# Dense first layer with products alternating between two PSUM banks, and rounding, lo parts and cuts issued one or two products later

## The chip, the cores and the metric

One core of one Trainium2 chip. The number is device time in microseconds; lower is better. Five engines run their own instruction streams in order and wait for one another through semaphores: TensorE (PE; its weight loads PEld), VectorE (DVE), ScalarE (ACT), GpSimd (POOL) and SyncE (SP), which here mostly starts DMAs.

## The reference

Three layers in a row, float32 throughout, with large inputs (most are drawn 8 times wider), so that products are computed in split precision.

```python
k_p, v_p = mean of k, v over groups of 8 positions            # pooled attention
attn = softmax(q @ k_p.T / sqrt(D)) @ v_p                     # 8 x 8 heads, 576 x 64
x = attn as (4608, 512)
e = argmax(x @ w_gate); x = gate * sigmoid(...) * relu(x @ w1[e]) @ w2[e]   # 8 experts
h = x @ w_in                                                  # (4608, 512) @ (512, 2048)
r = maximum(h, 0); g = s * (r * r) + b
out = g @ w_out                                               # (4608, 2048) @ (2048, 512)
```

The last three lines are the dense stage, the one that is mostly changed.

## The kernel before

The program runs attention, then the expert stage, then the dense stage. Every engine's order is written out by hand, in the order of the Python calls; nothing moves instructions afterwards.

**Split precision.** A float32 factor is kept as a rounded part (hi, made on ScalarE by an activation with `Copy`) and a rest (lo, made on VectorE by subtracting hi). A product is three matmuls: hi x hi, hi x lo, lo x hi. `split` (L806 to L808) makes one pair; where the raw values are features or weights, the text calls it a cut.

**Dense stage** (class `Dense`). Tokens come in 6 groups of 768, the 2048 hidden features in 8 pairs of 128 columns, so there are 48 steps, counted `n = 8 q + p`. The first layer of a step is Winograd's form of a 2 x 2 block product: seven products of 384 columns (six matmuls each, lines 1339 to 1341) instead of eight. They take seven sums of feature blocks (`xt`, cut once a group) and seven sums of weight blocks (`ws`, in DRAM, read back through a ring of 8 slots). The table `PROD` gives, for each product, the weight sum, the PSUM bank and whether the bank starts anew. After a product, `post` reads its bank: `keep` copies it (ScalarE, L1345, for products 0, 2 and 3), or `finish` completes one quarter of the hidden values: addition of a kept block on VectorE (L1359) or Relu on ScalarE (L1355), square (L1361 or L1357), scale and bias on VectorE (L1362), rounding on ScalarE (L1368), and the lo part (L1350) at the next finish. The second layer of step n-1 runs as 12 chunks (three matmuls of 512 columns each, L1315 to L1317) placed after the products of step n by `AFTER`; they accumulate in six further PSUM banks (`po`) and are copied and stored by POOL's indirect DMA at the end of a group (L1324 to L1327).

The features of the next group are prepared meanwhile: `load` (transposing DMAs, L1229), `join` on POOL (two halves put together, L1248, and a multiplication by the token's scale, L1252), the sums on POOL (L1255), and seven `cut`s in the group's last step and the next one's first. Two of POOL's four sums are made in `cut`, after the cuts that read the blocks they overwrite.

**Weights.** `Doubles.step` turns the 64-bit `w_in` and `w_out` into float32. In the expert stage it forms the sums of `w_in`, cuts them into `halves()`, one buffer, and in the next call stores that to `ws` from SP's queue (L925). Two pieces out of four end in such a cut. Twelve pieces of `w_out` are left for the first dense steps.

**End of the expert stage.** After slot 35 there may be more slots under conditions on the number of tiles; `ahead` issues POOL's joins and sums for the first group just before them. The gathers of later slots (L1012) follow on POOL.

## Time and profile before

| | us |
|---|---|
| three runs, median (range) | 1550.47 (1550.26 to 1553.07) |
| profiled execution | 1553.91 |
| its span, first to last instruction | 1552.0 |
| TensorE busy | 1441.0 (93%) |
| VectorE / ScalarE / POOL busy | 919.1 / 536.8 / 563.9 (59% / 35% / 36%) |
| mean granted TensorE clock | 0.983 |

Matmuls overlap in the pipeline and their ends are modelled, so the busy share of TensorE says little by itself; the time between starts and the waits say more. Attention lasts to about 300 us, the expert stage to about 711 us, the dense stage's first product starts at 712.8 us. Steps are counted by their products: line 1339 has 672 matmuls, 14 in each of 48 steps.

### The profile page before, as it was taken

The page shows a single profiled execution, that of the slowest core. Times are in us where ns is not written, and L with a number is a line of the kernel's source. Part 1 is how long each engine was busy: PE and PEld are TensorE (multiplying, and loading weights), DVE is VectorE, ACT ScalarE, POOL GpSimd, SP SyncE. Part 2 cuts the span into 40 slices and gives each one's busy share as a digit, 9 for nine tenths or more (in the row PEclk, how much of TensorE's full clock was granted, in tenths as well). Part 3 has the DMA queues.
Part 4 walks back from the last instruction along what each step waited for, and adds up shares of the span by engine and source line. Part 5 has one row for each costly group of instructions (what it writes and reads, how often), then busy time and mean ns, then how long its engine had stood idle before and what let it go on. Part 6 is the DMA issues. An engine that isn't in the chain of part 4 may idle for free.

```text
span 1552.0 us, 23038 instructions
## 1 busy us (share of the span) xinstructions
PE 1441.0 (93%) x7552; PEld 1251.2 (81%) x7552; DVE 919.1 (59%) x1779; ACT 536.8 (35%) x1087; POOL 563.9 (36%) x718
## 2 busy tenths in 40 slices
PE   5899999999899999996999899899989989998995
PEld 4888978887788877885778788788878978887894
DVE  6688875668556574227756554655665565465452
ACT  3566533445344453223322322322232232232221
POOL 5996333434565565153333132133123113311001
PEclk9999999999999999998999999999999999999998
DMA  9994352487667686646354554375456436444431
GB/s 248 288 277 139 130 198 76 130 219 241 183 156 232 162 259 185 63 98 205 116 143 119 142 157 118 106 184 133 117 160 142 117 108 176 127 117 141 116 107 41
DMA packets 203120, 239.69 MB, mean 154 GB/s; under 512 B 66718, under 2 KB 114078, under 8 KB 202974
## 3 DMA queue, kind: packets, MB, share of 16 engines
q1 hardware_dynamic: 195502, 217.22, 51.4%
q0 software_dynamic: 7472, 20.75, 5.0%
q8 instruction: 63, 1.03, 0.3%
q14 instruction: 83, 0.68, 0.2%
HBM read 184.65 MB, written 43.83 MB: 147 GB/s over the span
## 4 chain that ended last, share of the span: by engine, by line
PE 37%; DVE 10%; ACT 4%; issue 2%; DMA 1%; POOLq 0%; DVEq 0%; ACTq 0%
PE po L1317 6%; PE po L1316 6%; PE bank L1339 6%; PE po L1315 6%; PE bank L1340 6%; PE bank L1341 6%; DVE wb L1350 3%; DVE r L1362 2%; DVE r L1361 2%; DVE r L1359 1%; ACT wb L1368 1%; ACT wa L807 1%; DVE wa L808 1%; ACT held L1345 1%; DMA out<-yo,kp_pos 1%
## 5 line engine op out<-in xcount | busy, mean ns | idle before, releaser
L1368 ACT ACTIVATE wb<-r 128x384 fp32r<-128x384 f32 x192 | 100.8, 525 | 512.8 <-DVE r L1362 512.8
L1359 DVE TENSOR_TENSOR r<-bank,held 128x384 f32<-128x384 f32 x144 | 80.0, 555 | 256.5 <-PE bank L1341 248.4
L1317 PE MATMUL po<-wo,wb 128*128 128x512 f32 x576 | 230.1, 400 | 0.0
L1316 PE MATMUL po<-wo,wb 128*128 128x512 f32 x576 | 229.2, 398 | 0.0
L1315 PE MATMUL po<-wo,wb 128*128 128x512 f32 x576 | 225.8, 392 | 0.0
L1339 PE MATMUL bank<-wa,ring 128*128 128x384 f32 x480 | 168.1, 350 | 47.1 <-ACT held L1345 31.3
L1062 PE MATMUL py<-wb,hh 128*128 128x512 f32 x624 | 193.6, 394 | 4.7 <-PEq L1141 3.8
L1340 PE MATMUL bank<-wa,ring 128*128 128x384 f32 x480 | 163.8, 341 | 0.0
L1341 PE MATMUL bank<-wa,ring 128*128 128x384 f32 x480 | 162.8, 339 | 0.0
L1339 PEld LDWEIGHTS bank<-wa,ring 128*128 128x128 f32 x480 | 91.3, 190 | 78.1 <-ACT held L1345 48.1
L1062 PEld LDWEIGHTS py<-wb,hh 128*128 128x128 f32 x624 | 118.7, 190 | 30.2 <-issue 4.0
L1350 DVE TENSOR_TENSOR wb<-r,wb 128x384 fp32r<-128x384 f32 x192 | 128.0, 666 | 24.8 <-ACT wb L1368 21.4
L1327 POOL DMA_INDIRECT out<-yo,kp_pos x36 | 35.2, 979 | 290.6 <-ACT yo L1326 190.6
L934 POOL TENSOR_SCALAR dt<-dt 128x256 f32<-128x256 f32 x64 | 69.0, 1078 | 167.7 <-DVE dt L933 140.6
L1317 PEld LDWEIGHTS po<-wo,wb 128*128 128x128 f32 x576 | 108.8, 189 | 23.6
L1031 PE MATMUL ph<-wa,xh 128*128 128x512 f32 x312 | 126.2, 405 | 0.0
L1032 PE MATMUL ph<-wa,xh 128*128 128x512 f32 x312 | 122.3, 392 | 1.2 <-DVE wa L808 1.0
L1033 PE MATMUL ph<-wa,xl 128*128 128x512 f32 x312 | 122.3, 392 | 0.0
L1062 PE MATMUL py<-wb,hl 128*128 128x512 f32 x312 | 120.5, 390 | 0.0
L1315 PEld LDWEIGHTS po<-wo,wb 128*128 128x128 f32 x576 | 109.2, 190 | 11.7
L1316 PEld LDWEIGHTS po<-wo,wb 128*128 128x128 f32 x576 | 109.0, 189 | 11.6
L1255 POOL TENSOR_TENSOR next<-next 128x768 f32<-128x768 f32 x20 | 40.5, 2024 | 192.6 <-DVE wa L808 192.2
(243 smaller groups left out, 2933.1 us busy)
## 6 DMA issues: line engine op xcount, KB each, us to landing
ring<-ws SPq DMA_DIRECT2D x336, 256.0 KB, 2.7
wr<-in_moe_w SPq DMA_DIRECT2D x72, 512.0 KB, 6.7
ws<-wf SPq DMA_DIRECT2D x16, 896.0 KB, 6.1
ys<-y SPq DMA_DIRECT2D x38, 256.0 KB, 5.4
xd<-x SPq DMA_DIRECT2D x36, 256.0 KB, 3.8
q<-in_q SPq DMA_DIRECT2D x16, 512.0 KB, 8.2
vr<-in_v SPq DMA_DIRECT2D x8, 1024.0 KB, 10.8
dx<-in_moe_w_out SPq DMA_DIRECT2D x32, 256.0 KB, 4.4
```

The costliest lines, as they stand in the source:

```text
L1031: nc.tensor.matmul(ph, lhsT=xh[:, k], rhs=wh[:, k, s], start=k == 0, stop=False)
L1032: nc.tensor.matmul(ph, lhsT=xh[:, k], rhs=wl[:, k, s], start=False, stop=False)
L1033: nc.tensor.matmul(ph, lhsT=xl[:, k], rhs=wh[:, k, s], start=False, stop=k == 3)
L1062: nc.tensor.matmul(py, lhsT=a, rhs=w, start=j == 0, stop=j == len(steps) - 1)
L1315: nc.tensor.matmul(o, lhsT=gh[:, s], rhs=wh, start=first, stop=False)
L1316: nc.tensor.matmul(o, lhsT=gh[:, s], rhs=wl, start=False, stop=False)
L1317: nc.tensor.matmul(o, lhsT=gl[:, s], rhs=wh, start=False, stop=last)
L1339: nc.tensor.matmul(bank[b], lhsT=w[:, 0, k], rhs=xh[:, k], start=f, stop=False, skip_group_check=True)
L1340: nc.tensor.matmul(bank[b], lhsT=w[:, 0, k], rhs=xl[:, k], start=False, stop=False, skip_group_check=True)
L1341: nc.tensor.matmul(bank[b], lhsT=w[:, 1, k], rhs=xh[:, k], start=False, stop=False, skip_group_check=True)
L1350: nc.vector.tensor_tensor(out=gl, in0=r, in1=gh.bitcast(F32), op=ALU.subtract)
L1368: nc.scalar.activation(out=gh, in_=r, func=AF.Copy)
```

## The change

Products alternate between the two banks, and which of the two a step begins with alternates from step to step; the order of products 3 to 6 is changed (quarter 12 now comes before 21). Work that follows a read of a bank goes through a list: activations are issued after the next product (`later`, `due`), VectorE's part one product after that, ahead of what reads that product's bank. Scale and bias move from VectorE to a ScalarE activation (`Identity`). For groups 1 to 5, joins go from POOL to ScalarE (copies) and VectorE (multiplications), sums from POOL to VectorE; the sums get three buffers, and all four are made before the cuts. The pieces of `w_out` start one step later. In the expert stage the weight sums get two buffers and their stores go out from ScalarE's queue. The last step's chunks go through the quarters one after another.

```diff
--- before.py
+++ after.py
@@ -922,7 +922,7 @@
         self.n += 1
         while self.stores:
             c, r = self.stores.pop(0)
-            nc.sync.dma_start(out=self.ws[c][:, :, :, r], in_=self.halves())
+            nc.scalar.dma_start(out=self.ws[c][:, :, :, r], in_=self.halves(r))
         self.load(n + AHEAD)
         if n < self.end:
             x = self.x[n]
@@ -960,7 +960,7 @@
         if self.begin <= m < self.end:
             w, r, c = self.pieces[m]
             if w and r >= 2:
-                o = self.halves()
+                o = self.halves(r % 2)
                 split(nc, o[:, :, 0].bitcast(F32R), o[:, :, 1].bitcast(F32R), self.blocks(r % 2)[:, 1:])
                 self.stores.append((c, r % 2))
 
...
@@ -1198,7 +1198,7 @@
 RING = 8
 
 
-PROD = [(0, 0, True), (2, 1, True), (4, 0, False), (5, 0, False), (3, 1, True), (1, 0, False), (6, 1, False)]
+PROD = [(0, 0, True), (2, 1, True), (4, 0, False), (3, 1, True), (5, 0, False), (6, 1, False), (1, 0, False)]
 AFTER = [2, 2, 2, 2, 2, 1, 1]
 KEYS = [("11", 1, 0), ("22", 0, 3), ("21", 0, 0), ("12", 1, 3)]
 
...
-    def join(self, g, k):
+    def join_steps(self, g, k, copy, eng):
 
         f = self.xf[:, k]
         o = f.bitcast(U16).rearrange("p (n w) -> p n w", w=2)
-        for w, t in enumerate(self.t.pop((g, k))):
-            self.nc.gpsimd.tensor_copy(out=o[:, :, w], in_=t)
+        copies = [lambda w=w, t=t: copy(out=o[:, :, w], in_=t) for w, t in enumerate(self.t.pop((g, k)))]
         n = GT * P // 3
-        for i, b in enumerate(self.scale[g]):
-            h = f[:, i * n:i * n + n]
-            self.nc.gpsimd.tensor_tensor(out=h, in0=h, in1=b.bitcast(F32), op=ALU.mult)
-
-    def sub(self, o, x, y):
-        self.nc.gpsimd.tensor_tensor(out=o, in0=x, in1=y, op=ALU.subtract)
+        scales = [
+            lambda h=f[:, i * n:i * n + n], b=b: eng.tensor_tensor(out=h, in0=h, in1=b.bitcast(F32), op=ALU.mult)
+            for i, b in enumerate(self.scale[g])
+        ]
+        return copies, scales
+
+    def sum_steps(self, eng):
+
+
+        b, z = self.block, self.z
+        return [
+            lambda o=o, x=x, y=y: eng.tensor_tensor(out=o, in0=x, in1=y, op=ALU.subtract)
+            for o, x, y in (
+                (b(0, 1), b(0, 1), b(0, 0)), (z[0], b(1, 1), b(0, 1)), (z[1], z[0], b(0, 0)), (z[2], b(1, 0), z[0])
+            )
+        ]
+
+    def cut_steps(self, j):
+
+        b, z = self.block, self.z
+        raw = [b(0, 0), b(1, 0), z[0], b(0, 1), z[1], b(1, 1), z[2]][j]
+        hi, lo = self.xt[j]
+        return (
+            lambda: self.nc.scalar.activation(out=hi, in_=raw, func=AF.Copy),
+            lambda: self.nc.vector.tensor_tensor(out=lo, in0=raw, in1=hi.bitcast(F32), op=ALU.subtract),
+        )
+
+    def later(self, acts, vecs, n=1):
+
+
+        self.acts += [(self.i + 1, f) for f in acts]
+        self.vecs += [(self.i + 2 + j // n, f) for j, f in enumerate(vecs)]
+
+    def due(self, i):
+        self.i = i
+        for queue in (self.acts, self.vecs):
+            now = [f for t, f in queue if t <= i]
+            queue[:] = [x for x in queue if x[0] > i]
+            for f in now:
+                f()
+
+    def join(self, g, k):
+        self.later(*self.join_steps(g, k, self.nc.scalar.copy, self.nc.vector), n=3)
 
     def sums(self):
-
-
-        self.sub(self.block(0, 1), self.block(0, 1), self.block(0, 0))
-        self.sub(self.z, self.block(1, 1), self.block(0, 1))
-
-    def cut(self, i):
-
-        b = self.block
-        split(self.nc, *self.xt[i], [b(0, 0), b(1, 0), self.z, b(0, 0), b(0, 1), b(1, 0), b(1, 1)][i])
-        if i == 0:
-            self.sub(b(0, 0), self.z, b(0, 0))
-        if i == 1:
-            self.sub(b(1, 0), b(1, 0), self.z)
+        self.later([], self.sum_steps(self.nc.vector))
+
+    def cut(self, j):
+        hi, lo = self.cut_steps(j)
+        self.later([hi], [lo])
+
+    def join_now(self, g, k):
+        copies, scales = self.join_steps(g, k, self.nc.gpsimd.tensor_copy, self.nc.gpsimd)
+        for f in copies + scales:
+            f()
+
+    def sums_now(self):
+        for f in self.sum_steps(self.nc.gpsimd):
+            f()
+
+    def cut_now(self, js):
+        for j in js:
+            for f in self.cut_steps(j):
+                f()
 
...
@@ -1332,57 +1377,55 @@
         def product(i):
             n, j = divmod(i, 7)
             m, b, start = PROD[j]
+            o = bank[(b + n) % 2]
             w = self.ring[i % RING]
             xh, xl = self.xt[j]
             for k in range(2):
                 f = start and k == 0
-                nc.tensor.matmul(bank[b], lhsT=w[:, 0, k], rhs=xh[:, k], start=f, stop=False, skip_group_check=True)
...
+                nc.tensor.matmul(o, lhsT=w[:, 0, k], rhs=xh[:, k], start=f, stop=False, skip_group_check=True)
...
+        def keep(o, j):
+            held[j] = p4.tile([P, HT], F32, tag="held", name="held")
+            nc.scalar.copy(out=held[j], in_=o)
+
+        def finish(n, o, key, other):
             r = p4.tile([P, HT], F32, tag="r", name="r")
             if other is None:
-                nc.scalar.activation(out=r, in_=bank[0], func=AF.Relu)
-                low()
+                nc.scalar.activation(out=r, in_=o, func=AF.Relu)
                 nc.vector.tensor_tensor(out=r, in0=r, in1=r, op=ALU.mult)
             else:
-                nc.vector.tensor_tensor(out=r, in0=bank[1], in1=held[other], op=ALU.add)
-                low()
+                nc.vector.tensor_tensor(out=r, in0=o, in1=held[other], op=ALU.add)
                 nc.vector.scalar_tensor_tensor(out=r, in0=r, scalar=0.0, in1=r, op0=ALU.max, op1=ALU.mult)
-            nc.vector.tensor_scalar(
-                out=r, in0=r, scalar1=s_b[:, 0:1], scalar2=s_b[:, 1:2], op0=ALU.mult, op1=ALU.add
-            )
             t = self.gt[self.gn % len(self.gt)]
             self.gn += 1
             gh, gl = t[:, 0:HT], t[:, HT:2 * HT]
-            nc.scalar.activation(out=gh, in_=r, func=AF.Copy)
-            lows.append((r, gh, gl))
             gs[n, key] = gh, gl
+            self.later(
+                [
+                    lambda: nc.scalar.activation(
+                        out=r, in_=r, func=AF.Identity, scale=s_b[:, 0:1], bias=s_b[:, 1:2]
+                    ),
+                    lambda: nc.scalar.activation(out=gh, in_=r, func=AF.Copy),
+                ],
+                [lambda: nc.vector.tensor_tensor(out=gl, in0=r, in1=gh.bitcast(F32), op=ALU.subtract)],
+            )
 
         def post(n, j):
+            o = bank[(PROD[j][1] + n) % 2]
             if j in (0, 2, 3):
-                keep(j)
+                keep(o, j)
             else:
-                finish(n, *{1: ("11", 0), 4: ("22", 3), 5: ("21", None), 6: ("12", 2)}[j])
-
-        steps = list(range(NSTEP))
-        for n in steps:
-            q, p = divmod(n, NPAIR)
+                finish(n, o, *{1: ("11", 0), 4: ("22", 3), 5: ("12", 2), 6: ("21", None)}[j])
+
+        for n in range(NSTEP):
             todo = [(n - 1, *key, j) for key in KEYS for j in range(GT // 2)] if n else []
             for j in range(7):
                 i = 7 * n + j
                 self.weights(i + RING - 1)
                 product(i)
+                self.due(i)
                 post(n, j)
                 self.side(n, j)
                 for _ in range(1 if n == NSTEP - 1 else AFTER[j]):
@@ -1390,38 +1433,35 @@
                         chunk(*todo.pop(0))
             while todo:
                 chunk(*todo.pop(0))
-        low()
+        self.due(7 * NSTEP + 2)
         n = NSTEP - 1
-        for a, b in ((0, 2), (1, 3)):
+        for a in (0, 2, 1, 3):
             for j in range(GT // 2):
-                for key in (KEYS[a], KEYS[b]):
-                    chunk(n, *key, j)
+                chunk(n, *KEYS[a], j)
 
     def side(self, n, j):
 
 
         q, p = divmod(n, NPAIR)
-        if q == 0 and p < 4 and j % 2 == 0:
+        if q == 0 and 1 <= p < 5 and j % 2 == 0:
             self.db.step()
-        if q and (p, j) == (0, 0):
-            self.cut(6)
         if q + 1 == NGRP:
             return
         if n == 0 and j == 6:
-            self.features(self.next)
+            n = GT * P
+            self.features(self.next, [self.next[:, 4 * n:5 * n], self.extra[:, 0:n], self.extra[:, n:2 * n]])
         plan = PLAN0 if q == 0 else PLAN
         for what, k in plan.get((p, j), []):
             getattr(self, what)(*((q + 1, k) if what in ("load", "join") else () if k is None else (k,)))
+        if p == NPAIR - 1:
+            self.cut(j)
 
 
 PLAN = {(1, 1): [("load", 0)], (2, 1): [("load", 1)], (3, 1): [("load", 2)], (4, 1): [("load", 3)],
         (2, 5): [("join", 0)], (3, 5): [("join", 1)], (4, 5): [("join", 2)], (5, 5): [("join", 3)],
-        (6, 3): [("sums", None)]}
+        (6, 1): [("sums", None)]}
 PLAN0 = {(4, 1): [("load", 0)], (4, 4): [("load", 1)], (5, 1): [("join", 0), ("load", 2)],
-         (5, 4): [("join", 1), ("load", 3)], (6, 0): [("join", 2)], (6, 3): [("join", 3)], (6, 6): [("sums", None)]}
-for _p in (PLAN, PLAN0):
-    for _j in range(1, 7):
-        _p[7, _j] = [("cut", _j - 1)]
+         (5, 4): [("join", 1), ("load", 3)], (6, 0): [("join", 2)], (6, 2): [("join", 3)], (6, 4): [("sums", None)]}
 
 
 @with_exitstack
@@ -1517,27 +1557,25 @@
         elif 0 <= k < 3:
             dn.load(0, k)
         elif k == 3:
-            dn.features(db.wf)
-            dn.join(0, 0)
+            dn.features(db.wf, [db.wf[:, i * GT * P:(i + 1) * GT * P] for i in range(4, 7)])
+            dn.join_now(0, 0)
             dn.load(0, 3)
         elif k == 4:
             for k in range(1, 4):
-                dn.join(0, k)
-            dn.sums()
+                dn.join_now(0, k)
+            dn.sums_now()
 
...
         def tail():
             raw.close()
             dn.open(ctx.enter_context(tc.tile_pool(name="dn2", bufs=1, side="right")))
             db.run(db.end, len(db.pieces))
-            for i in range(5):
-                dn.cut(i)
+            dn.cut_now(range(5))

...
```

Three places in the order of instructions. ScalarE in an ordinary step of the dense stage, before, from the last rounding (L1368) of the step ahead of it to its own product 5; `bank_10538` is bank 0:

```order
L1368 ACTIVATE wb_2828<-r 128x384 x2
L1345 COPY held<-bank_10538 128x384
L1368 ACTIVATE wb_2828<-r 128x384
L1345 COPY held<-bank_10538 128x384 x2
L1368 ACTIVATE wb_2828<-r 128x384
L1355 ACTIVATE r<-bank_10538 128x384
```

and in the changed kernel, one step from its product 0 to its product 6 (L1391 is `keep`, L1396 the Relu, L1407 scale and bias, L1410 the rounding; `bank_10542` and `bank_10543` are the two banks):

```order
L1391 COPY held<-bank_10543 128x384
L1407 ACTIVATE r<-r,s_b 128x384
L1410 ACTIVATE wb_2828<-r 128x384
L1391 COPY held<-bank_10543 128x384
L1391 COPY held<-bank_10542 128x384
L1407 ACTIVATE r<-r,s_b 128x384
L1410 ACTIVATE wb_2828<-r 128x384
L1407 ACTIVATE r<-r,s_b 128x384
L1410 ACTIVATE wb_2828<-r 128x384
L1396 ACTIVATE r<-bank_10543 128x384
```

All copies used one bank; now both are read. A rounding stands behind the next product's place instead of in its own finish, with scale and bias ahead of it.

POOL at the end of the expert stage, before (the sums of the first group, the branch to a conditional slot, and that slot's gather):

```order
L1255 TENSOR_TENSOR wf<-wf 128x2x384
L1255 TENSOR_TENSOR wf<-wf 128x768
L1141 COMPARE_AND_BRANCH
L859 UNCONDITIONAL_BRANCH
L1012 DMA xg_2857<-xd,kp_idx 128x512
```

and in the changed kernel:

```order
L1261 TENSOR_TENSOR wf<-wf 128x2x384
L1261 TENSOR_TENSOR wf<-wf 128x768 x3
L1141 COMPARE_AND_BRANCH
L859 UNCONDITIONAL_BRANCH
L1012 DMA xg_2857<-xd,kp_idx 128x512
```

Two sums moved ahead of the gather; they stood in the tail, between the cuts.

ScalarE in a slot of the expert stage, as the difference between the two (L925 is the store of the weight sums, L932 the first instruction of a piece, L807 a cut of hidden values):

```order
 L859 UNCONDITIONAL_BRANCH x2
 L1009 COPY y<-py 128x512
+L925 DMA ws_105<-wf 1792x1x128
 L932 ACTIVATE dx<-dx 128x256
 L807 ACTIVATE hh_2865<-th 128x512
```

The store's issue now stands in ScalarE's order, ahead of the piece of the next call.

## Rows read from the trace of the kernel before

**Rows 1.** Windows of the dense stage (start:end, length, busy by engine, PEclk, DMA, GB/s)
```profile
712.76:855.07 142.31, 126.21 (x588) 109.89 (x589) 92.32 (x166) 40.33 (x91) 49.76 (x48) 0.95 0.52 146
855.07:990.30 135.23, 129.11 (x624) 113.40 (x624) 75.61 (x131) 36.24 (x74) 31.35 (x30) 0.99 0.51 136
990.30:1123.83 133.53, 127.63 (x625) 112.17 (x625) 75.49 (x131) 36.26 (x74) 31.46 (x30) 1.00 0.53 137
1123.83:1257.38 133.55, 127.85 (x624) 112.15 (x625) 76.66 (x131) 36.26 (x74) 31.52 (x30) 1.00 0.53 137
1257.38:1393.78 136.40, 129.58 (x624) 113.36 (x624) 77.92 (x131) 36.26 (x74) 32.05 (x30) 0.99 0.49 134
1393.78:1508.90 115.12, 110.72 (x546) 98.56 (x547) 59.44 (x116) 30.05 (x63) 5.84 (x6) 1.00 0.46 126
1430.47:1508.90 78.43, 78.43 (x391) 70.48 (x390) 37.47 (x76) 18.47 (x41) 0.72 (x1) 1.00 0.45 121
```
**Rows 2.** TensorE's waits in the dense stage: total us, times, longest
```profile
PE bank L1339 <- ACT held L1345: 31.3, 24, 3.7
PE bank L1339 <- DVE r L1359: 10.9, 6, 2.1
PE bank L1339 <- ACT r L1355: 3.2, 6, 1.0
```
**Rows 3.** Timeline in step 8: start, us, engine, line, [idle before <- releaser]
```profile
861.75 0.83 ACT L807 ACTIVATE wb<-next 128x768 fp32r<-128x768 f32 x1
862.62 0.96 DVE L808 TENSOR_TENSOR wb<-next,wb 128x768 fp32r<-128x768 f32 x1 [1.33 <-ACT wb L807]
866.64 0.52 ACT L1368 ACTIVATE wb<-r 128x384 fp32r<-128x384 f32 x1 [2.94 <-DVE r L1362]
867.07 0.46 ACT L1345 COPY held<-bank 128x384 f32<-128x384 f32 x1
867.58 0.44 PE L1339 MATMUL bank<-wa,ring 128*128 128x384 f32 x1 [1.86 <-ACT held L1345]
```
**Rows 4.** Groups by line and shape, dense stage: count, busy us, mean ns, idle
```profile
L1362 DVE TENSOR_SCALAR r<-r,s_b 128x384 f32<-128x384 f32 x192 | 102.7, 535 | 7.0
L808 DVE TENSOR_TENSOR wa<-next,wa 128x768 fp32r<-128x768 f32 x25 | 32.0, 1296 | 20.6 <-ACT wa L807 20.6
L808 DVE TENSOR_TENSOR wb<-next,wb 128x768 fp32r<-128x768 f32 x10 | 9.6, 958 | 7.4 <-ACT wb L807 7.2
L1368 ACT ACTIVATE wb<-r 128x384 fp32r<-128x384 f32 x192 | 100.8, 525 | 512.8 <-DVE r L1362 512.8
L1345 ACT COPY held<-bank 128x384 f32<-128x384 f32 x144 | 67.3, 467 | 74.7 <-PE bank L1341 74.7
L1248 POOL COPY next<-dy 128x768 uint16<-128x768 uint16 x40 | 43.9, 1144 | 122.7 <-DMA dy<-ys 122.7
```
**Rows 5.** Waits in the expert stage from 300 us on: total us, times, longest
```profile
ACT wf L807 <- DMA ws<-wf: 40.1, 6, 12.4
PE th L1045 <- ACT hs L1035: 7.4, 3, 3.8
```
**Rows 6.** Window behind one of these waits, columns as in rows 1
```profile
418.00:421.40 3.40, 3.17 (x13) 2.77 (x14) 3.15 (x7) 2.73 (x7) 0.30 (x1) 0.50 0.02 5
```
**Rows 7.** SP's stores of the weight sums: count, ns min/median/max of the issue
```profile
L925 SPq DMA_DIRECT2D ws<-wf x16: 533/554/1137, 409.2 to 632.8; - x16
```
**Rows 8.** Chain of waits at the end: start, us, what
```profile
1527.11 0.60 ACT yo L1326
1527.97 2.67 DMA out<-yo,kp_pos
...
1531.41 2.66 DMA out<-yo,kp_pos
```
**Rows 9.** Timeline at the end of the expert stage
```profile
690.57 3.77 POOL L1255 TENSOR_TENSOR wf<-wf 128x768 f32<-128x768 f32 x2
...
698.97 0.66 PE L1021 MATMUL pt<-ident,xg 128*128 128x128 f32 x4 [1.24 <-DMA xg<-xd,kp_idx]
```

30 lines of the change are left out of this document (12 added, 18 removed).

## The prediction

> **What bounds the kernel now.** I read the windows first, then TensorE's waits, then the timeline at the worst wait, then the costs by line.
>
> The windows cut the dense stage at the starts of steps 0, 8, 16, 24, 32, 40 and 47 [rows 1]. The last row, steps 42 to 46, shows TensorE busy for all of its 78.43 us: an undisturbed step takes 15.69 us. It streams 42 matmuls of 384 columns and 36 of 512, 34,560 columns, so by columns a product (2304) takes 1.05 us and a chunk (1536) 0.70 us; both are estimates from that row. Step 0 has no chunks, which makes it 7.3 us. Eight steps should take 125.5 us, group 0 (step 0 and seven more) 117.1 us, steps 40 to 46 109.8 us. The windows show 142.3, 135.2, 133.5, 133.6, 136.4 and 115.1 us. The losses are 25.2, 9.7, 8.0, 8.1, 10.9 and 5.3 us: **67 us**, all that any change to this stage's order can win. The granted clock of 0.95 in group 0 says that a part of it is time at the lower level (1.2 GHz).
>
> What TensorE waits for is the first matmul of a product, and there the reader of its PSUM bank: ScalarE's copy 31.3 us, VectorE's addition 10.9 us, ScalarE's Relu 3.2 us [rows 2]. The rest of the 67 us is refilling the pipeline and the lower clock that follows the waits. The reader is late because it stands behind other work. At 866.64 ScalarE had waited 2.94 us in L1368 for VectorE's `r`; the copy L1345 that frees the bank stood behind it in ScalarE's order and began at 867.07; TensorE's product started at 867.58 after 1.86 us. VectorE, in turn, had waited 1.33 us in a cut for ScalarE [rows 3]. Two engines that work in order wait for one another in turn, and TensorE for both.
>
> **The change, part by part, dense stage.** Products now alternate between two banks. Before, product 3 followed product 2 into one bank with two chunks, 1.4 us, between; now a bank is read while another product runs, so the reader has 0.7 + 1.05 + 0.7 = 2.45 us at the short end (products 4 to 6) and 3.85 us elsewhere. In step 0, without chunks, it has 1.05 us against a copy of 0.47 us or an addition of about 0.56 us.
>
> Rounding, lo part and cut come one or two products later, so what a queue meets ahead of a reader has its inputs ready. The queues must then only keep up. VectorE: steps 42 to 46 show 37.47 us busy, 7.5 us a step [rows 1]; four L1362 of 0.53 us leave it [rows 4], so about 5.4 us. ScalarE: 18.47 / 5 = 3.7 us, plus four scale-and-bias activations. The trace has none; L1368 of the same shape takes 0.525 us and is the value I take, L1345's 0.467 us is the low end and POOL's 1.14 us for a copy of twice the columns [rows 4] the high end. That is 5.8 us, at most 8.3, of 15.69.
>
> In a group's last step seven cuts come on top. VectorE's take 0.96 us where POOL rests (L808 into wb) and 1.30 us on average where POOL works beside it (L808 into wa) [rows 4]. POOL's joins and sums go to ScalarE and VectorE, so I take 0.96: 5.4 + 6.7 = 12.1 us; ScalarE 5.8 + 7 x 0.84 = 11.7 us, L807's 0.84 us read from the timeline's 0.83 at 861.75 [rows 3]. Both fit in 15.69. The joins that move (two copies, three multiplications, once in each of four steps) cost ScalarE 0.6 to 2.3 us a step, the low end one 0.60 us output copy at the trace's end [rows 8] and the high end POOL's 2 x 1.14, and VectorE at most 3 x 0.96 us; I take 2 us each, in steps with room. The four sums of 768 columns go one to a product, at VectorE's 0.96 to 1.30 us.
>
> On POOL's port: the two L808 rows differ by 0.34 us at one shape. The Trainium skill ("SBUF — State Buffer", section "Who interferes with whom") says that a VectorE instruction with two SBUF inputs contends with a GpSimd instruction that reads SBUF, and that ScalarE waits on nobody. The trace agrees for these rows (0.96 and 1.30 us); by the rule the later cuts are all near 0.96, and without it the last step's VectorE load is 5.4 + 9.1 = 14.5 us, still under 15.69.
>
> What stays: small delays in step 0, and output stores. These land one after another 3.4 us apart (1527.97, 1531.41) [rows 8]; the sixth copy of a group needs the second's buffer, so VectorE can stand there some microseconds in the first step of a group, against a reader with 3.85 us. I leave 6 us of the 67. The bounds: about 2 us (jitter, no waits) and half of the 67. **Dense: -61 us.**
>
> **The weight sums.** In the expert stage ScalarE's rounding of the sums L807 waits 40.1 us in six places for the store out of the single buffer; behind it stands the Relu that TensorE's transposes wait for, 7.4 us in three places [rows 5]. After two of these the clock stands at 0.50 for 3.4 us [rows 6], so each costs 1.7 us more. With two buffers the store has two more steps to land: -(7.4 + 3.4) = -10.8 us. The store's issue moves to ScalarE: 0.55 us in SP's queue, 1.14 at most [rows 7], 16 of them. It waits for VectorE's lo part, cut half a slot earlier. ScalarE issues behind the Relu or ahead of cuts that TensorE needs a slot later, so I cost it at nothing; without that cover 16 x 0.55 = 8.8 us, and below, a little gain because SP's queue is free of a wait. **Experts: -11 us.**
>
> **What it adds.** First, POOL now makes four sums ahead of the conditional slots, where it made two; two took 3.77 us. Behind them in POOL's order stands a gather whose tile TensorE already waits for (1.24 us at 698.97) [rows 9]. Two more sums put it 3.8 us later: **+3.8 us**, in full, since TensorE's branch and the last expert's matmuls follow it. The two sums that left the tail release a cut that product 3 waited for; that gain is in group 0's 25.2 us. Second, the last step's chunks go 11, 21, 22, 12. The first output tile is complete after four chunks, not two, 1.4 us later, and the chain from its copy at 1527.11 on is stores one behind another [rows 8]: **+1.4 us**.
>
> Sum: -61 - 11 + 3.8 + 1.4 = -67 us from the profiled execution's 1553.9 us (span 1552.0 and 1.9 around it): 1487 us. That execution lies 3.4 us above the median of the runs, 1550.5; on the median's scale I say **1484 us**.
>
> **Rivals.** *VectorE becomes the bound in cutting steps.* If copies, stores or DMA and not POOL stretched the cuts, and the four sums and the yo copies fall on the same products, its 14.5 us passes 15.69 in steps 7, 15, 23, 31, 39 and the next step starts late by about 2 us each: +10, 1494 us. For it: 1.30 us is the mean. Against it: POOL is idle there now. Chance 14%.
>
> *ScalarE's queue holds the reader again.* Each finish now puts two activations, 1.05 us, ahead of a copy, and in last steps a cut of 0.84 as well: 2.4 us with the copy, against 1.75 us between products 5 and 6. If the delay adds up over neighbouring products, half the waits stay: +28, 1512 us. Against it: the readers' 2.45 us of room, and 2.24 us between products on average. 8%.
>
> *Slower: the clock.* If switching banks each product makes a short pause that sends the clock to its lower level once a step, every step pays what the stretch at 418 us paid, 1.7 us [rows 6]: 48 x 1.7 = 82 us, 1566 us. It decides from about 40 such stretches on. The windows speak against it: chunks already walk over six banks, and steps 42 to 46 keep 1.00 [rows 1]. A page bears on this: the Trainium skill ("TensorE: Matmul & The Clock Gate", section "A second HAM failure mode: psum-queue depth-cycling") tells of a kernel whose cycling through PSUM banks made TensorE pause between groups and its clock swing between two levels. 4%.
>
> *It does not do what it says*: another wait of the same size stands behind the bank's, and only the experts' gain is left against the 5 us added: 1545 us, or, with that gain at its low end of 6 us, 1550, inside the 0.2% (3 us) that a measurement of this kernel can tell from no change. 2%.
>
> **How the numbers follow.** The forecast has 72%, with its own range of 1474 to 1492 (the dense residual from 2 to 12 us, the experts from -6 to -13, the gather from 0 to +5). The range 1471 to 1502 takes in the second case and the better end of the first, and leaves out the third and the slower ones. Faster by over 0.2%: 0.94; within: 0.02; slower: 0.04.
>
> **What would show it.** Right: the windows of a full group near 126 us; TensorE's waits for `held` and `r` under 5 us in total; no ScalarE wait for `ws` stores, and no lower clock in the expert stage or after step 1; the wait for `xg` before the tail near 5 us; POOL empty in the dense stage but for stores. Wrong: groups above 130 us with VectorE or ScalarE busy throughout their last step, waits of ScalarE for VectorE's lo part at L925, or a granted clock below 1.00 in most steps.

## The result, and the profile after

The changed kernel takes 1482.8 us (median of four runs, 1477.9 to 1491.6) against 1550.4 us: a ratio of 0.957, 95% interval 0.952 to 0.961. The forecast was 1484 us. The profiled run of the changed kernel is the slowest of its four: 1491.6 us, span 1489.8. Why its runs lie 14 us apart is a part of what follows. One run of a kernel further down, the one with only the dense part (2025.9 us at a mean granted clock of 0.654), is left out of its median and interval.

The windows of the dense stage, cut at the starts of steps 0, 8, 16, 24, 32, 40 and 47, and then steps 42 to 46, with the columns of [rows 1]:

```profile
714.00:832.39 118.39, 117.51 (x588) 106.07 (x589) 77.68 (x156) 69.47 (x131) 22.95 (x24) 1.00 0.65 181
832.39:958.39 126.00, 126.00 (x625) 112.50 (x624) 62.68 (x115) 66.45 (x115) 6.31 (x6) 1.00 0.55 145
958.39:1084.39 126.00, 126.00 (x625) 112.49 (x624) 62.68 (x115) 66.45 (x115) 6.16 (x6) 1.00 0.56 145
1084.39:1210.39 126.00, 126.00 (x625) 112.48 (x624) 62.80 (x115) 66.53 (x115) 6.16 (x6) 1.00 0.56 145
1210.39:1336.39 126.00, 126.00 (x625) 112.50 (x624) 62.77 (x115) 66.48 (x115) 6.17 (x6) 1.00 0.54 145
1336.39:1446.20 109.81, 109.81 (x548) 98.68 (x546) 45.65 (x83) 48.94 (x90) 5.85 (x6) 1.00 0.48 132
1367.77:1446.20 78.43, 78.43 (x392) 70.49 (x390) 29.78 (x55) 32.76 (x61) 0.94 (x1) 1.00 0.44 122
```

In each row from step 8 on TensorE is busy for the whole window. Every full group takes 126.00 us where [rows 1] show 133.5 to 136.4; the granted clock is 1.00 in all rows. From the first product to the last chunk the stage took 820.7 us and takes 755.9: **-64.9 us**. TensorE's waits in it, as in [rows 2] (there 45 us in readers of a bank):

```profile
PE bank L1385 <- DMA ring<-ws: 1.4, 1, 1.4
PE bank L1385 <- ACT held L1391: 0.9, 1, 0.9
```

Some of the groups by line, as in [rows 4]; L1274 is a cut's lo part and stands where L808 stood, L1412 is a product's lo part:

```profile
L1407 ACT ACTIVATE r<-r,s_b 128x384 f32<-128x384 f32 x192 | 136.1, 709 | 281.5 <-DVE r L1400 253.3 <-DVE r L1397 28.2
L1412 DVE TENSOR_TENSOR wb<-r,wb 128x384 fp32r<-128x384 f32 x192 | 106.9, 559 | 68.6 <-ACT wb L1410 68.6
L1274 DVE TENSOR_TENSOR wa<-next,wa 128x768 fp32r<-128x768 f32 x20 | 19.1, 954 | 1.4 <-ACT wa L1273 1.0
```

VectorE's cut into `wa` takes 0.95 us, where [rows 4] have 1.30. ScalarE still waits for VectorE's `r` (281 us in all), but no reader of a bank stands behind that wait at a time when TensorE needs it.

The expert stage went otherwise. ScalarE no longer waits for `ws` stores in L807 [rows 5]; these are its waits and TensorE's from 300 us on that take their place:

```profile
ACT dx L932 <- SPq L859: 32.2, 4, 9.9
```
```profile
PE py L1062 <- ACTq L859: 4.4, 2, 2.4
PE py L1062 <- DVE wb L808: 2.8, 3, 1.1
PE py L1062 <- ACT wb L807: 1.8, 1, 1.8
```

L932 is what follows the store's issue on ScalarE. The second longest of these waits, 9.34 us, shows what it is. The timeline of SP, ScalarE and TensorE around it:

```profile
581.47 3.03 SPq L832 DMA_DIRECT2D wr<-in_moe_w  x4
...
582.33 0.58 ACT L1009 COPY y<-py 128x512 uint16<-128x512 uint16 x1
...
592.25 0.43 ACT L932 ACTIVATE dx<-dx 128x256 int32<-128x256 uint32 x1 [9.34 <-SPq L859]
...
592.59 1.06 ACT L807 ACTIVATE hh<-th 128x512 fp32r<-128x512 f32 x2
...
593.75 0.65 PE L1062 MATMUL py<-wb,hh 128*128 128x512 f32 x1 [2.42 <-ACTq L859]
```

ScalarE ends its copy at 582.91 and does nothing until 592.25; TensorE then waits for the hidden values (`hh`) that ScalarE rounds behind it. In between stands only the issue of the store at L925:

```profile
L925 ACTq EVENT_SEMAPHORE  x16: 17/17/17, 409.9 to 633.1; - x16
L925 ACTq DMA_DIRECT2D ws<-wf x16: 525/526/583, 410.0 to 633.2; - x16
```

Each issue has a semaphore wait ahead of it. In the trace's semaphore records the one that ends at 591.64 waits for a counter of landed DMAs. There are eight such counters, which the issues of SP and of ScalarE use in turn, and the last DMA on this one before the store is a part of the next expert's weights (`wr`, the second of four, issued by SP at 582.15). But that part had landed at 587.75. The counter was still short of what the store waits for, because these loads stand under a condition (L859, the expert changes): where it is false, SP's sequencer passes over the loads and raises their counters itself, one after another, each after a wait for the earlier DMAs on it. Here SP waited for the third and the fourth part of `wr` on two other counters (landed at 589.19 and 591.42) and raised the store's counter at 591.61, 0.03 us before ScalarE's wait ended. The view of L859 from 581 to 592 us has SP's five waits at that line and, under those who waited for it, ScalarE:

```profile
L859 SPq EVENT_SEMAPHORE  x5: 17/17/17, 586.8 to 591.6; - x5
  ACT dx L932: 9.3, 1
```

In six of the 16 places the last DMA on the store's counter is a load of `wr`, and ScalarE stands there for 9.3, 2.9, 6.8, 3.4, 5.1 and 8.8 us, 36.2 in all; in the other ten it is at most 0.6 us. Five of the six ended with a raise by SP, up to 8.5 us behind the landing on that counter, and one (3.4 us) with the landing itself. [rows 5] had 40.1 us, in six places. The slots that suffer (numbers 16, 28, 29 and 30 of the 12.25 us each) lost 12.9 us before and lose 16.2 us in this run; slots 12 and 15, which lie ahead of the first store, lose 3.2 us more (3.4 before). The clock falls behind the waits as in [rows 6]:

```profile
594.00:600.80 6.80, 6.18 (x15) 4.53 (x15) 4.49 (x8) 2.79 (x5) 4.63 (x9) 0.50 0.81 183
```

At the end of the expert stage the rows that answer to [rows 9] are these, POOL's four sums, its gather and the transposes of what was gathered, which don't wait:

```profile
689.27 7.47 POOL L1261 TENSOR_TENSOR wf<-wf 128x768 f32<-128x768 f32 x4
...
696.89 1.02 POOL L1012 DMA_INDIRECT xg<-xd,kp_idx  x1
...
701.89 0.60 PE L1021 MATMUL pt<-ident,xg 128*128 128x128 f32 x4
```

And the end of the chain, as in [rows 8]:

```profile
1464.86 0.59 ACT yo L1371
...
1465.72 2.67 DMA out<-yo,kp_pos
...
1469.16 2.67 DMA out<-yo,kp_pos
```

The span adds up by parts: slot 38, the last, starts 4.3 us later than before (690.01 against 685.68; 1.5 of it was there at the start of slot 1, ahead of all that was changed), the way from there to the first product is 3.1 us shorter (23.99 against 27.08), the dense stage 64.9 shorter, what follows the last matmul 1.4 longer (19.9 against 18.5): -62.3 us; the spans differ by 62.2.

### The profile page after: what moved, and what is told of

Its sections match the earlier page's. It is cut to its first block, busy times and chain, and to the rows that moved or that the text cites. A ratio compares the mean times of both kernels' runs of the same rounds, so it can differ in the third digit from the quotient of the medians.

```text
span 1489.8 us, 22917 instructions
## 1 busy us (share of the span) xinstructions
PE 1428.0 (96%) x7552; PEld 1251.4 (84%) x7552; DVE 827.5 (56%) x1667; ACT 708.9 (48%) x1319; POOL 429.7 (29%) x598
## 4 chain that ended last, share of the span: by engine, by line
PE 50%; DMA 1%; issue 1%; ACT 0%; POOLq 0%; DVE 0%; SPq 0%; DVEq 0%
PE po L1362 9%; PE po L1361 9%; PE po L1360 9%; PE bank L1385 8%; PE bank L1386 8%; PE bank L1387 8%; DMA out<-yo,kp_pos 1%; DMA ring<-ws 0%; POOLq L1604 0%; ACT r L1407 0%; ACT yo L1371 0%; DVE r L1399 0%; DVE r L1400 0%; ACT wb L1410 0%; SPq L1336 0%
## 5 line engine op out<-in xcount | busy, mean ns | idle before, releaser
L1407 ACT ACTIVATE r<-r,s_b 128x384 f32<-128x384 f32 x192 | 136.1, 709 | 281.5 <-DVE r L1400 253.3
L1062 PE MATMUL py<-wb,hh 128*128 128x512 f32 x624 | 198.0, 400 | 13.2 <-ACTq L859 4.4
L1385 PE MATMUL bank<-wa,ring 128*128 128x384 f32 x480 | 162.3, 338 | 2.3 <-DMA ring<-ws 1.4
L1386 PE MATMUL bank<-wa,ring 128*128 128x384 f32 x480 | 162.1, 338 | 0.0
L1387 PE MATMUL bank<-wa,ring 128*128 128x384 f32 x480 | 161.0, 335 | 0.0
L1412 DVE TENSOR_TENSOR wb<-r,wb 128x384 fp32r<-128x384 f32 x192 | 106.9, 559 | 68.6 <-ACT wb L1410 68.6
L807 ACT ACTIVATE hh<-th 128x512 fp32r<-128x512 f32 x78 | 42.4, 594 | 150.3 <-PE th L1045 150.3
L808 DVE TENSOR_TENSOR hl<-th,hh 128x512 fp32r<-128x512 f32 x78 | 50.1, 684 | 105.8 <-ACT hh L807 105.8
```

The source lines that it names most:

```text
L1062: nc.tensor.matmul(py, lhsT=a, rhs=w, start=j == 0, stop=j == len(steps) - 1)
L1385: nc.tensor.matmul(o, lhsT=w[:, 0, k], rhs=xh[:, k], start=f, stop=False, skip_group_check=True)
L1386: nc.tensor.matmul(o, lhsT=w[:, 0, k], rhs=xl[:, k], start=False, stop=False, skip_group_check=True)
L1387: nc.tensor.matmul(o, lhsT=w[:, 1, k], rhs=xh[:, k], start=False, stop=False, skip_group_check=True)
L1407: lambda: nc.scalar.activation(out=r, in_=r, func=AF.Identity, scale=s_b[:, 0:1], bias=s_b[:, 1:2]),
L1412: [lambda: nc.vector.tensor_tensor(out=gl, in0=r, in1=gh.bitcast(F32), op=ALU.subtract)],
```

## The experiments

Kernels that are listed together ran on one chip beside the kernel before (1545.8 us there in the first four, 1548.4 in the next four, 1548.0 in the last three). Medians differ by several us between chips, so I compare within one.

**Where the expert part's gain went: four kernels.** The changed kernel again:

> The changed kernel again, with nothing changed, for a second profile and for its spread on the chip on which the others run. Both theories: 1483 us, single runs between 1476 and 1492. If the spread comes from the expert stage, as I think, the dense stage takes 756 us from its first product to its last chunk in this profile too, and only the start of the first product moves.

Measured 1478.2 us (1473.6 to 1481.1), ratio 0.955 [0.953, 0.958]; six long holds at L925 again, 33 us in all; dense stage 755.9 us. Its slots from 1 on lose 9.6 us in all, where those of the first profile lose 19.4 and those of the kernel before 16.6. With the stores back on SP's queue, two buffers kept:

```diff
-nc.scalar.dma_start(out=self.ws[c][:, :, :, r], in_=self.halves(r))
+nc.sync.dma_start(out=self.ws[c][:, :, :, r], in_=self.halves(r))
```

> The changed kernel with the stores of the weight sums issued from SP's queue again; the two buffers stay. Theory A: in the changed kernel ScalarE stands at the store's issue (L925, gaps of 36 us in total) because the store's completion semaphore was last used by a load of the next expert's weights, which has not landed; on SP the same wait holds nobody that TensorE needs. Then ScalarE has no gap there, no wait for ws in L807 either, TensorE's waits in the expert stage shrink by about 11 us, and the time is 1469 to 1475. Rival B: the slots in which the expert changes are held by the weight loads themselves, whoever issues the store; then TensorE's waits there stay (about 12 us) with another releaser, and the time stays at 1480 to 1486.

Measured 1474.5 us (1473.5 to 1475.9), ratio 0.954 [0.951, 0.956], in theory A's range; the slots of its profile lose nothing. Its runs lie within 2.4 us, those of the changed kernel within 7.6, and five of those six are slower than all of these. (That the load "has not landed" holds for one hold in six: the others waited for SP's raise, as above.) With the store on SP's queue and one buffer, as before the change (only the dense part is left of it):

```diff
-nc.scalar.dma_start(out=self.ws[c][:, :, :, r], in_=self.halves(r))
+nc.sync.dma_start(out=self.ws[c][:, :, :, r], in_=self.halves(0))
-                o = self.halves(r % 2)
+                o = self.halves(0)
```

> The changed kernel with the expert stage's part undone: one buffer of weight sums and stores from SP. Theory A (that part gave nothing, since the wait only moved from L807 to L925): 1480 to 1488, the same as the changed kernel within 4 us; ScalarE waits about 40 us in L807 for ws stores, as before. Rival B (two buffers are worth the 11 us that I forecast, and something else cost them): 1492 to 1496. The dense stage takes 756 us by both.

Measured 1483.6 us (1479.5 to 1485.1 in five runs), ratio 0.958 [0.955, 0.961]; ScalarE waits 35.7 us in L807 again, and the slots lose 10.4. The time lies in theory A's range, but 5.4 us above the changed kernel on this chip and not within its 4, so the expert part did give something. Last, the expert part alone on the kernel before:

> The kernel before with the expert stage's part alone: two buffers of weight sums, stores from ScalarE's queue; the dense stage as before. Theory A: 1546 to 1554, no difference from before that counts, gaps of 30 to 40 us in total at L925 in place of the 40 us in L807. Rival B: 1537 to 1541.

Measured 1542.4 us against 1545.8, ratio 0.998 [0.996, 1.000], between the ranges of the two theories; six long holds at L925, 31 us; the dense stage's loss stays (66.2 us).

The windows 395 to 440 and 550 to 610 us, where the stores fall, of the kernel with only the dense part and of the one with stores on SP's queue (columns as in [rows 1]):

```profile
395.00:440.00 45.00, 41.65 (x195) 34.49 (x194) 21.41 (x41) 13.99 (x26) 23.66 (x30) 0.96 0.68 177
550.00:610.00 60.00, 56.94 (x274) 47.42 (x273) 40.45 (x61) 25.69 (x40) 40.84 (x44) 0.97 0.80 246
```
```profile
395.00:440.00 45.00, 45.00 (x224) 37.79 (x223) 25.14 (x44) 16.61 (x31) 26.34 (x32) 1.00 0.75 208
550.00:610.00 60.00, 60.00 (x296) 50.41 (x295) 40.38 (x59) 26.75 (x43) 42.64 (x46) 1.00 0.77 234
```

In the second TensorE is busy throughout at full clock, and each slot takes 12.25 us. The two kernels differ by the buffer alone: it is worth 1483.6 - 1474.5 = 9.1 us. The issue on ScalarE gives 3.7 of them back (1478.2; the intervals of these two ratios overlap), so that the expert part as made is worth 5.4 us there.

**What removes the dense stage's waits: order or banks.** In one kernel the banks alternate, but roundings, lo parts, cuts, joins and sums are issued at once, in the step of their product:

```diff
-        self.acts += [(self.i + 1, f) for f in acts]
-        self.vecs += [(self.i + 2 + j // n, f) for j, f in enumerate(vecs)]
+        for f in acts + vecs:
+            f()
```

> The alternation of banks, the order of the products and both buffers of weight sums stay; roundings, lo parts, cuts, joins and sums are issued in the step of the product that they belong to, as soon as its reader is issued. Theory A (the issue order is what removes the waits: a queue never meets, ahead of a bank's reader, an instruction whose input is still being made): the waits between ScalarE and VectorE come back, above all in each group's last step with its seven cuts, and TensorE waits 15 to 45 us for readers in the dense stage; 1495 to 1525 us. Theory B (the alternation gives the readers so much room, 2.45 us and more, that their delay by a wait on another engine no longer reaches TensorE): TensorE waits under 5 us in the dense stage, and the time is within 5 us of the unchanged changed kernel's 1478 to 1483.

Measured 1523.5 us (1519.2 to 1523.9), ratio 0.983 [0.978, 0.988]. TensorE's waits in its dense stage, and one of them in the timeline:

```profile
PE bank L1385 <- DVE r L1399: 12.3, 13, 3.8
PE bank L1385 <- ACT r L1396: 8.7, 21, 0.5
PE bank L1385 <- ACT held L1391: 8.2, 25, 0.8
```
```profile
807.45 0.53 ACT L1410 ACTIVATE wb<-r 128x384 fp32r<-128x384 f32 x1
808.01 0.56 DVE L1412 TENSOR_TENSOR wb<-r,wb 128x384 fp32r<-128x384 f32 x1 [1.34 <-ACT wb L1410]
808.49 1.94 DVE L1261 TENSOR_TENSOR next<-next 128x768 f32<-128x768 f32 x2
810.46 1.83 DVE L1261 TENSOR_TENSOR extra<-next 128x768 f32<-128x768 f32 x2
812.21 0.55 DVE L1399 TENSOR_TENSOR r<-bank,held 128x384 f32<-128x384 f32 x1
...
812.81 0.62 PE L1385 MATMUL bank<-wa,ring 128*128 128x384 f32 x1 [3.79 <-DVE r L1399]
```

VectorE first stands 1.34 us for ScalarE's rounding of a value that it has itself squared just before, then makes four sums, and only then reads the bank: TensorE waits 3.79 us. That is [rows 3] again, with two banks. The stage loses 49.2 us against TensorE's own pace, where the kernel before loses 68.3 and the changed one 3.4.

In the other kernel the later issue stays, and products keep their old order and their old bank (`o = bank[b]`):

```diff
-PROD = [(0, 0, True), (2, 1, True), (4, 0, False), (3, 1, True), (5, 0, False), (6, 1, False), (1, 0, False)]
+PROD = [(0, 0, True), (2, 1, True), (4, 0, False), (5, 0, False), (3, 1, True), (1, 0, False), (6, 1, False)]
```

> The later issue stays; products go back to their old order and each to its old bank, so that product 3 follows product 2 into one bank with two chunks (1.4 us) between, and product 5 follows 4, and 0 of the next step follows 6. Theory A (issue order is what counts): the copies are issued before the deferred work of the next product and find the queue free, 0.5 us after the product at the latest; TensorE waits under 8 us in all, half of it in step 0 where no chunks stand between; 1478 to 1490 us. Theory B (room is what counts): with 0.7 to 1.4 us of room each of the two activations of a finish (1.05 to 1.23 us) that stands ahead of a copy makes TensorE late by some tenths of a us, two or three times a step: 20 to 45 us in the dense stage, 1500 to 1525 us.

Measured 1489.8 us (1488.6 to 1494.3), ratio 0.962 [0.957, 0.967]. The stage loses 14.1 us. Its waits for ScalarE's copy, and the longest one outside step 0:

```profile
PE bank L1385 <- ACT held L1391: 6.0, 12, 1.9
```
```profile
784.70 0.53 ACT L1410 ACTIVATE wb<-r 128x384 fp32r<-128x384 f32 x1
785.13 1.95 ACT L1248 COPY next<-dy 128x768 uint16<-128x768 uint16 x2
...
786.95 0.47 ACT L1391 COPY held<-bank 128x384 f32<-128x384 f32 x1
...
787.47 0.44 PE L1385 MATMUL bank<-wa,ring 128*128 128x384 f32 x1 [0.98 <-ACT held L1391]
```

Here the copy doesn't stand behind a wait for another engine; it merely has a join's two copies (1.95 us) ahead of it, more than the 1.4 us of two chunks. (In step 0 it does: scale and bias ahead of it waits 1.80 us for VectorE, and TensorE 1.92 us.) So, taken out of the changed kernel, the later issue costs 49.2 - 3.4 = 45.8 us and the alternation of banks 14.1 - 3.4 = 10.7. Measured from the kernel before, the first kernel gains 68.3 - 49.2 = 19.1 us and the second 54.2, of 64.9 together. By its ranges theory A holds: 1523.5 us lies in that for the first kernel (1495 to 1525), where TensorE waits 29 us for readers, and 1489.8 at the upper end of that for the second (1478 to 1490); theory B misses both. But the banks' 10.7 us are real, too.

Some cautions. The gains from the kernel before are those of packages: both kernels keep scale and bias on ScalarE, the joins and sums on ScalarE and VectorE, the three buffers of sums and the later start of `w_out`, and only the joins and sums are undone in a run by themselves (the next one). The kernel that issues at once also makes the four sums in one piece, which the changed kernel spreads over products, and its lo parts at once, which the kernel before left to the next finish; its 49.2 us are those of this order, not only of the delay by a product.

**POOL beside VectorE.** Joins and sums of groups 1 to 5 back on POOL, cuts left where they are:

```diff
-        self.later(*self.join_steps(g, k, self.nc.scalar.copy, self.nc.vector), n=3)
+        self.join_now(g, k)
-        self.later([], self.sum_steps(self.nc.vector))
+        self.sums_now()
```

> The joins and the sums of groups 1 to 5 go back to POOL (in the same step as before the change); cuts stay on ScalarE and VectorE. If VectorE was slowed by POOL's reads, VectorE's cuts and lo parts beside POOL take 1.3 and 0.67 us in place of 0.96 and 0.56, but VectorE loses 20 sums and 60 multiplications (some 70 us over the stage), so it has more room than in the changed kernel: dense stage 755 to 760 us, the time within 3 us of the changed kernel's. If the joins' place on ScalarE and VectorE were what removes the waits, the dense stage goes up by 10 us or more.

Measured 1475.7 us (1474.5 to 1481.6), ratio 0.953 [0.948, 0.958]; the dense stage is 753.9 us, 2.0 shorter, and a little below the range expected. Three groups by line:

```profile
L1412 DVE TENSOR_TENSOR wb<-r,wb 128x384 fp32r<-128x384 f32 x192 | 124.7, 652 | 84.0 <-ACT wb L1410 84.0
L1261 POOL TENSOR_TENSOR extra<-next 128x768 f32<-128x768 f32 x10 | 20.7, 2092 | 0.4
L1274 DVE TENSOR_TENSOR wa<-next,wa 128x768 fp32r<-128x768 f32 x20 | 19.1, 955 | 1.6 <-ACT wa L1273 1.2
```

VectorE's lo part is slower on average (0.652 us for 0.559), as expected, but its cuts are not: 0.955 us where 1.3 was expected, since POOL ends its sums before the cuts begin (at 900.3 and 933.9 us in group 1). Where joins and sums stand is not what removes the waits.

**The end, and the gather.** Stores on SP's queue and, in addition, the last chunks in pairs as before the change:

```diff
-        for a in (0, 2, 1, 3):
+        for a, b in ((0, 2), (1, 3)):
             for j in range(GT // 2):
-                chunk(n, *KEYS[a], j)
+                for key in (KEYS[a], KEYS[b]):
+                    chunk(n, *key, j)
```

> The weight sums' stores stay on SP's queue (two buffers), and the last step's chunks go in pairs again (11 with 21, then 22 with 12), so that the first output tile is complete after two chunks. I expect the expert stage of the run with the stores on SP's queue (every slot 12.24 us, 1474.5 us) and a tail after the last matmul of 18.5 in place of 19.9 us: 1472 to 1474 us. If the tail is bound by the last tile and not by the first, the time stays at 1474 to 1476.

Measured 1473.5 us (1470.9 to 1478.0), ratio 0.951 [0.947, 0.954], on another chip than the kernel without the pairs, so the medians don't tell 1.4 us apart. In its trace the time behind the last matmul is 18.6 us, against 19.9. And its profiled run shows what the changed kernel's doesn't, the gather late:

```profile
675.87 7.45 POOL L1261 TENSOR_TENSOR wf<-wf 128x768 f32<-128x768 f32 x4
683.47 1.02 POOL L1012 DMA_INDIRECT xg<-xd,kp_idx  x1
...
687.34 1.12 PE L1021 MATMUL pt<-ident,xg 128*128 128x128 f32 x4 [4.30 <-DMA xg<-xd,kp_idx]
```

On the last chip the changed kernel ran beside two more. Its own expectation and result:

> The changed kernel unchanged, as the measure on this chip for the two kernels run beside it: 1476 to 1484 us, its runs spread over 5 us or more, and again some of ScalarE's issues at L925 late by 2 to 9 us behind a load of the next expert's weights. In the entry POOL's joins start early against TensorE, and TensorE waits under 1 us for the gathered tokens.

Measured 1478.5 us (1476.6 to 1481.4), ratio 0.956 [0.953, 0.958]; six holds of 2.4 to 8.3 us, the slots lose 5.2, and TensorE doesn't wait for gathered tokens. Next, the kernel with SP's stores and pairs, with two of the four sums behind the gather again (`sums_now(0, 2)` where four stood, `sums_now(2, 4)` ahead of the tail's cuts):

> The kernel with the stores on SP's queue and the last chunks in pairs; in addition two of the four sums of group 0 (z[1] and z[2]) go behind the last gather in POOL's order again, ahead of the tail's cuts. With the stores on SP's queue POOL's first sum stood 1.4 us behind slot 38's start in one profile and 4.9 us in the other, with all four sums ahead of the gather, which was issued at 9.0 and 12.5 us; TensorE waited 0.8 and 4.9 us for it, and the way from slot 38 to the first product was 25.6 and 30.7 us. Theory A (the gather waits for POOL's order, the prediction's step): with two sums behind it, it is issued 3.7 us earlier against the first sum, 5.1 to 8.8 us behind slot 38, TensorE waits 0 to 1.5 us for it, the way is 24 to 27.5 us, and the time is 1 to 3.5 us under that of four sums (1473.5): 1470 to 1473. Theory B (the gather is late by its own transfer or the branch): the way stays at 25.6 to 30.7 us and the time at 1473.5.

Measured 1471.3 us (1469.3 to 1474.4), ratio 0.951 [0.948, 0.953]. Its rows:

```profile
672.72 3.77 POOL L1261 TENSOR_TENSOR wf<-wf 128x768 f32<-128x768 f32 x2
676.64 1.02 POOL L1012 DMA_INDIRECT xg<-xd,kp_idx  x1
...
682.20 0.60 PE L1021 MATMUL pt<-ident,xg 128*128 128x128 f32 x4
```

The gather is issued 3.9 us behind the first sum, not 7.6, and the transposes don't wait. (The expectation's 4.9 us of waiting in the other profile are 4.3 in the trace.) The way from slot 38 to the first product is 24.6 us. In the kernel with only the dense part the joins started alike (first sum 2.2 us behind slot 38, here 2.4) and all four sums stood ahead of the gather: it left at 9.8 us, TensorE waited 1.6 us, and the way was 27.0. The traces bear theory A out; the time doesn't decide it, since against the kernel before the ratio is that of four sums (0.951 both). Last, all of it with POOL's joins:

> Stores on SP's queue, last chunks in pairs, two sums behind the gather, and the joins and sums of groups 1 to 5 back on POOL. From the runs so far the last part takes 2 us from the dense stage (excess over TensorE's own pace 1.5 in place of 3.5 us): 1468 to 1471 us, a ratio to the kernel before of 0.948 to 0.951, the fastest of all. If POOL's joins slow VectorE's readers beside them, the dense stage is no shorter than 755.9 us and the time is that of the run without this part.

Measured 1471.1 us (1468.9 to 1472.5), ratio 0.950 [0.948, 0.953], dense stage 753.9 us. Level with the kernel beside it: the 2 us are in the stage but not in the medians (one slot of its profile loses 1.5 us). Both are some 7 us faster than the changed kernel on the same chip, and have the lowest medians of all; their ratios and that of the kernel with SP's stores and pairs are the same within the intervals.

## Why the prediction was right, point by point

**Dense stage, -61: right, measured -64.9.** The mechanism is the one named, and the two experiments show that both parts count: without the later issue 45.8 us come back, without the banks 10.7. I left 6 us and 3.4 stay, 1.3 of them in step 0, where the copy is late by 0.9 us; the output stores that I feared don't appear. The shortest room of a reader, 2.45 us, is that of product 5 alone; by `AFTER`, products 4 and 6 have 3.15. What queues do in a plain step is 6.0 us on VectorE and 6.6 on ScalarE (29.78 and 32.76 over five steps), against 5.4 and 5.8; ScalarE's surplus is L1407, 0.709 us and not the 0.525 that I took from L1368, a row without a scale and a bias per partition. (The Trainium skill, "ScalarE: Activation LUTs", section "What ACT_TABLE_LOAD costs", adds about 93 ns for each such operand; two of them make an estimate of 0.525 + 0.186 = 0.711, and the trace agrees.) In a group's last step I had 12.1 and 11.7 us; step 15 (942.70 to 958.39) shows VectorE 10.48 and ScalarE 10.24 of 15.69, since the last cuts run over into the next step. So neither of the first two rivals came true. The clock rival didn't either: 1.00 in all windows, also with a switch of banks at each product. The pauses and the swinging clock that the Trainium skill tells of with cycling through banks ("TensorE: Matmul & The Clock Gate", section "A second HAM failure mode: psum-queue depth-cycling") don't show here: TensorE is busy for the whole of each window from step 8 on.

On POOL's port: with joins and sums on POOL, VectorE's lo part took 0.65 us on average and without them 0.56, while ScalarE's L1407 took 0.709 in both. The Trainium skill ("SBUF — State Buffer", section "Who interferes with whom") says that a VectorE instruction with two SBUF inputs contends with a GpSimd instruction that reads SBUF, and that ScalarE waits on nobody; the trace agrees. But I read the 1.30 us of [rows 4] wrongly, as POOL did not work beside all of these cuts. The kernel before has, as minimum, median and maximum in ns:

```profile
L808 DVE TENSOR_TENSOR wa<-next,wa x25: 945/959/2659, 845.6 to 1397.1; 128x768 fp32r<-128x768 f32 x25
```

Twenty of them took at most 0.96 us, and five, one in each group, that began 0.01 us behind a sum on POOL took 2.65. Where a cut began ahead of POOL's second sum it took 0.95, and the sum 2.5 in place of 1.85. The port didn't decide the time: VectorE has room for it.

**The weight sums, -11: mis-sized, and the failed step is the sentence on the store's issue.** I had it "ScalarE issues behind the Relu or ahead of cuts that TensorE needs a slot later, so I cost it at nothing", and looked at the issue's own 0.55 us and at its data, VectorE's lo part. What it waits for is neither: the lo part was done at 584.11 in the case shown, and the wait went on to 591.64. It is for a counter shared with SP's loads, which SP itself raises where it passes over a load. (The Trainium skill, "DMA: Bandwidth & Descriptors", section "Anatomy of one DMA — SWDGE (gpsimd) path", says that a DMA's semaphore wait takes place on the sequencer that issues it, before dispatch; the six holds on ScalarE, up to 9.3 us, agree.) The wait of L807 for the store became a wait of the issue for SP, on the same engine, ahead of the same work, and nearly as long (36.2 for 40.1 us). The buffer itself is worth 9.1 us, near the 10.8 priced; the issue's place gives 3.7 back, by the medians of one chip, and in the run profiled first more than all (slot 38 at +4.3 where -11 stood). In the second profile only slots 16 and 28 to 30 lose time, and each of them has a long hold; with the stores on SP no slot loses any in three profiles of four (1.5 us in the fourth). The three profiles of the changed kernel, runs of 1491.6, 1481.1 and 1476.8 us, lose 19.4, 9.6 and 5.2 us in their slots, so most of its spread arises in the expert stage. Not all spread does: the kernel with SP's stores and pairs, whose slots lose nothing, still ranges over 7.2 us. That it waits for the counter and not for its data is read from the semaphore records; no run changed the counter alone.

**The gather, +3.8: the cost is there, the wait mostly not.** Two more sums put the gather 3.7 us later behind the first sum (7.6 us against 3.9 in [rows 9]), as priced. But I took POOL's joins to start where they did, and in the changed kernel they started earlier against TensorE: the gather left 6.9 us behind slot 38's start and not 8.8, and TensorE waited for nothing. Where the joins start as before (first sum 4.9 us behind slot 38 in both [rows 9] and the kernel with pairs), the gather leaves at 12.5 us, TensorE waits 4.3 us in one piece, and the way to the first product is 30.7 us, 3.6 more than before: the term as forecast. Where they start early, two more sums cost nothing: the way is 24.5 us in the kernel before with the expert part alone (first sum 0.1 us ahead of slot 38, two sums) and 24.6 in the second profile of the changed kernel (0.1 us behind it, four sums). The joins wait for the transposing loads to land (11.1 us before, 5.4 in the changed kernel), and that shifts from run to run; the term is one of 0 to 4 us, and I should have given it as that.

**The tail, +1.4: right.** From the first output copy to the last chunk's matmul it was 6.4 us (1527.11 to 1533.48) and is 5.0 (1464.86 to 1469.87), and the end lies 19.9 instead of 18.5 us behind the last matmul; in pairs it is 18.6 again.

Of the signs that I named, those of the dense stage came (126.00 us a group, 0.9 us of waits for `held`); two of the others didn't: the clock still fell to 0.50 in the expert stage, and TensorE did not wait for `xg` in that profile.

That 1484 and 1482.8 lie so close is partly luck, as errors of both signs cancel. In the first profile the dense stage gave 4 us more than forecast and the way to it 7 more (3.1 shorter, where 3.8 longer was forecast), while slot 38 came 15 us later; by the medians of one chip the expert part fell some 6 us short. And 1482.8 is the median of runs that lie 14 us apart.

## What to carry to other kernels

Put ahead of a bank's reader, in its engine's order, only what is ready by then: in the changed kernel the later issue by a product or two is worth 46 us, and the second bank 11. Before a DMA's issue is moved to an engine that computes, ask what the issue itself waits for: a completion counter that it shares with another queue's loads stops that engine as surely as missing data, and where those loads are conditional, until the other queue's engine gets to raising the counter. A term that rests on a start which loads decide belongs into the range with both ends, not into the sum.

## What the runs showed of the hardware that I had not expected

- A DMA issued from ScalarE stood up to 9.3 us ahead of its 0.53 us issue, for a counter that it shares with SP's DMAs; up to 8.5 us of that came after the last DMA on the counter had landed, until SP, which had waited for other loads first, raised it. From SP's queue the same store cost TensorE nothing (no slot loses time in that profile).
- A subtraction of 128x768 takes POOL 1.9 to 2.1 us in the dense stage, and VectorE 0.95. A VectorE cut of that shape that began 0.01 us behind one on POOL took 2.65 us; an average of 1.30 hid five of these among 20 of 0.96.
